# Lower parts, copies and operand sums put behind the work that the next products wait for

## The chip, the cores and the metric

The kernel runs on one core of a Trainium2 chip. The metric is the device time of one execution in microseconds; the time of a kernel is the median over its runs. One further execution is recorded by the hardware profiler, and all rows below come from that one.

The engines are named as in the profile: PE is the tensor engine (PEld its weight loads), DVE the vector engine, ACT the scalar engine, POOL the GpSimd engine, and SP the engine from whose queue nearly all transfers are issued.

## The reference

A decayed linear attention over blocks of 64 tokens, and then a two-layer feed-forward with a squared ReLU, everything in float32:

```python
for b in range(nb):
    intra = np.einsum('bhic,bhjc->bhij', qb, kb) * Dmask[None]
    intra = np.einsum('bhij,bhjd->bhid', intra, vb)
    inter = np.einsum('bhid,bhde->bhie', qb * lam_pow[None], kv_state)
    out[:, :, sl] = intra + inter
    kb_dec = kb * rev_pow[None]
    kv_state = lam_block[None, :, None, None] * kv_state + np.einsum('bhsd,bhse->bhde', kb_dec, vb)
...
h = x @ w_in
r = np.maximum(h, 0.0)
g = r * r
return (g @ w_out).astype(np.float32)
```

There are 4 sequences of 768 tokens, 8 heads of width 64, and a hidden width of 2048.

## The kernel before

**Precision.** A float32 product is made of three fast products: each operand is split into a high part (rounded, written by ACT or by a cast) and a lower part (the operand minus its high part, written by DVE), and high x high, high x low and low x high are added up. The helpers come in pairs: `part_hi`/`part_lo`, `rows_hi`/`rows_lo`, `fold_hi`/`fold_lo`, `weigh_hi`/`weigh_lo`. The `_hi` half runs on ACT, the `_lo` half on DVE. The tensors `wh` and `wl` hold the high and the lower parts of the weights, and later, in the same rows, those of other operands.

**Tiling.** The 3072 tokens are 24 chunks of 128 tokens, six per sequence, or six slices of four chunks. Slices 0 and 1 go through the feed-forward directly: for each of 16 hidden blocks f, `hidden` makes twelve products into a PSUM bank `h`, `square` (ACT) and `rest` (DVE) make `gh` and `gl` of it, and `project` of the previous block adds twelve products into four PSUM banks `acc`, one for each chunk. After the last block the four banks are copied out (tile `o`, two banks to a tile) and written to the output.

Slices 2 to 5 are done with seven products for every eight (sums of blocks of the operands are multiplied in place of the blocks). `quad(n)`, n = 0 to 7, opens the first pass over chunks 8 to 15, `gather_all(2, ...)` projects it, `quad_all(n, ...)` and `gather_all(4, ...)` do the same for chunks 16 to 23. I call `quad(0)` the first opening and `quad_all(0, ...)` the second. In an opening the products are numbered 0 to 6; products 0 and 4 go to bank `pa`, 1, 3 and 5 to `pb`, 2 and 6 to `pd`. After product 1 DVE adds `pb` and `p1` (a copy of product 0), after product 3 it does so again, and after product 4 it adds `pd` to that sum. Product 3 may start only when the first sum has read `pb`, product 5 when the second has, product 6 when `pd` has been read. The operand rows of the seven products are sums over chunks: `even` (rows 0 to 3), `last` (4 and 5), `near` (6 to 9), `far` (10 to 13).

**What runs beside it.** Slice 1 is the stretch in which all the preparation happens. At every even f, `go(t, t + 1)` runs the attention of one of the chunks 8 to 15: on PE the products with the old state (`old_state(0)`, L446), the scores of the next chunk (L411, into two banks `h`), the second half of the old state (`old_state(1)`, L446 again), and the products with the masked scores and the news for the state (L426). Between the first and the second half of the old state stands a one-element ACT copy (`mark`, L462), which PE waits for. `masked_by_half` (DVE, tile `a`) then multiplies the new scores by the mask; the next `hidden` reuses a bank of those scores, so PE's next twelve products wait for it. Beside that, in the same steps, the weights are recombined (`weigh`: tiles `rec`, `sums`, `parts`) and written to DRAM (`ws`), and the output weights are folded (`fold`: the same tile names, written to `wt`). POOL scales q, k and the state (`scale_q` L403, `scale_k` L395, `fade_state` L503).

**What sets the order.** Nothing is reordered by a scheduler: each engine runs its instructions in the order in which the Python code issues them, and waits in that order. A tile of a pool takes over the place of the tile of its tag that was released first, and waits for whatever still uses that. The tiles `rec`, `sums`, `near`, `far` and `o` share two places (tag `A`).

The calls at which the work stands, in the loop over f in slice 1:

```python
        for _, lo, x in now:
            lo(*x)
        if f == NF - 1:
            x = far(*pair(3))
            for a in (x, last(*pair(3))):
                part(*a)
        if f == 0:
            fold_hi(NQ - 2, True)
            fold_lo(NQ - 2)
        project(*prev)
        prev = (1, f)
        if f % 2 == 0:
            go(t, t + 1)
```

Of the kernel before, what the change touches and what calls it, by code (L numbers as in the profile page):

```python
# [35 lines left out]
def body(ctx: ExitStack, tc: tile.TileContext, qT, kT, kvq, lam, w, out):  # L36
# [399 lines left out]

    def go(t, after, own=None):
        po, pn = (ps_acc, "acc") if own is not None else (ps_a, "att")
# [23 lines left out]
        nc.scalar.copy(mark[:, 2:3], o[0][0:1, c : c + 1])  # L462
        u = o
        if after is not None:
            scores_by_half(after, qo, qn)
# [11 lines left out]
        if after is not None:  # L477
            part_of[after] = u[1]
            masked_by_half(after, own)
        x = kept(t).rearrange("p (a two c) -> p a two c", two=2, c=C)  # L480
        for h in range(2):
# [5 lines left out]

    def state(t, second):

        if not second and t % NCB == NCB - 1:  # L490
            return
        u = part_of.pop(t)[:, NPR * D :].rearrange("p (a b) -> p a b", a=NPR)
        d = kv[:, :, D:] if second else kv[:, :, 0:D]
        if second and not t % NCB:
            V.tensor_copy(d, u)
        else:
            add(d, kvd, u)
        if not second or t % NCB < NCB - 1:
            fade_state(second)
# [35 lines left out]
    def project(m, f):  # L535
        gh, gl = g_of.pop((m, f))
        if f == 0:
            accs[m] = [ps_acc.tile([P, DM], F32, name="acc") for _ in range(G)]
# [8 lines left out]
        def low(i):  # L547
            cs = slice(i * C, (i + 1) * C)
            nc.tensor.matmul(accs[m][i], gl[:, cs], wh[:, j], start=False, stop=end)  # L549
            if end:  # L550
                if i % 2 == 0:
                    stage.append(wk.tile([P, 2, DM], F32, name="o", tag="A"))
                o = stage[-1][:, i % 2]
                if i % 2 and not m:
                    V.tensor_copy(o, accs[m][i])
                else:
                    nc.scalar.copy(o, accs[m][i])
                t = chunk(m, i)
                nc.sync.dma_start(out=out[t * C : (t + 1) * C, :], in_=o)

        for i in range(G):
            high(i)
            low(i)

    def new_x(m):
# [202 lines left out]

    def quad(n, prev):
        f, t = 2 * n, 4 * G + n  # L770
# [24 lines left out]
        if n:  # L795
            square_pair(n - 1)
        product(n, 1, pb, True, False)
        add(gs[0], pb, p1)
        for e, i in MOVES.get(n, ()):
            move(e, spare(i))  # L800
# [81 lines left out]
    def quad_all(n, then):  # L882
# [25 lines left out]
        product(n, 3, pb, False, False)  # L908
        add(u3, pb, p1)
        product(n, 4, pa, False, True)  # L910
        add(gs[1], pd, u3)
# [201 lines left out]
    def late():  # L1113
        rows_lo(2, GT[0][:, 2:4])
        rows_of(6, GT[3][:, 2:4])
        rows_of(4, GT[1][:, 2:4])

# [161 lines left out]
    def behind(f, t):  # L1279
        if f % 2:  # L1280
            state(t, False)
            scale_q(t + 1)

    def ahead(f, t):
        if f % 2:
            state(t + 1, True)
            scale_k(t + 2)

# [9 lines left out]
    def pair(i):  # L1298
        return i, first_t + 2 * i

    todo = {f + 1: [(weigh_hi, weigh_lo, (n,))] for n, f in enumerate(WEIGH)}
    todo.setdefault(2, []).append((lambda n: fold_hi(n, True), fold_lo, (NQ - 3,)))
# [4 lines left out]
    for f in range(NF):  # L1307
# [14 lines left out]
        ahead(f, t)  # L1322
        for _, lo, x in now:
            lo(*x)
        if f == NF - 1:
            x = far(*pair(3))
            for a in (x, last(*pair(3))):
                part(*a)
        if f == 0:
            fold_hi(NQ - 2, True)  # L1330
            fold_lo(NQ - 2)
        project(*prev)
        prev = (1, f)
        if f % 2 == 0:
            go(t, t + 1)
            if t == last_t:
# [19 lines left out]
    for n in range(NF // 2):  # L1356
        quad(n, prev)
    for i, x in enumerate(GT):
# [61 lines left out]
```

## Time and profile before

| what | value |
|---|---|
| median of 3 runs | 580.46 us (580.02 to 581.17) |
| the profiled execution | 579.66 us, of which the span from the first to the last instruction is 578.0 us |
| PE busy | 566.7 us (98%) |
| DVE busy | 443.6 us (77%) |
| ACT busy | 299.2 us (52%) |
| POOL busy | 97.8 us (17%) |
| granted clock of PE | 1.000 over the whole span |

How to read it: PE is busy nearly all the time, and the granted clock never falls. The busy time of PE is modelled from the starts of its instructions, so what can be won without removing products is in the moments when PE waits. The other engines have slack on average, but not at every place.

### The profile page before, as it was taken

The page shows a single profiled execution, that of the slowest core. Times are in us where ns is not written, and L with a number is a line of the kernel's source. Part 1 is how long each engine was busy: PE and PEld are TensorE (multiplying, and loading weights), DVE is VectorE, ACT ScalarE, POOL GpSimd, SP SyncE. Part 2 cuts the span into 40 slices and gives each one's busy share as a digit, 9 for nine tenths or more (in the row PEclk, how much of TensorE's full clock was granted, in tenths as well). Part 3 has the DMA queues.
Part 4 walks back from the last instruction along what each step waited for, and adds up shares of the span by engine and source line. Part 5 has one row for each costly group of instructions (what it writes and reads, how often), then busy time and mean ns, then how long its engine had stood idle before and what let it go on. Part 6 is the DMA issues. An engine that isn't in the chain of part 4 may idle for free.

```text
span 578.0 us, 13430 instructions
## 1 busy us (share of the span) xinstructions
PE 566.7 (98%) x5308; PEld 494.1 (85%) x5308; DVE 443.6 (77%) x732; ACT 299.2 (52%) x524; POOL 97.8 (17%) x106
## 2 busy tenths in 40 slices
PE   9998999999999999999999999999999999999996
PEld 7886888887888888788888799999978888999996
DVE  5999999986887677767784699696865456997933
ACT  3777877834555555556675784153323234551510
POOL 4420221432313232322333000000000000000000
PEclk9999999999999999999999999999999999999999
DMA  8857485436699887499999776699678676767863
GB/s 302 325 173 259 151 285 186 143 128 239 220 292 362 284 271 258 133 315 366 370 392 357 257 229 214 204 293 330 196 243 258 197 192 194 237 216 208 284 203 109
DMA packets 87325, 142.69 MB, mean 247 GB/s; under 512 B 7776, under 2 KB 40544, under 8 KB 87264
## 3 DMA queue, kind: packets, MB, share of 16 engines
q1 hardware_dynamic: 82624, 136.61, 71.8%
q10 hardware_dynamic: 4640, 5.24, 2.5%
q8 instruction: 42, 0.69, 0.5%
q14 instruction: 19, 0.16, 0.1%
HBM read 106.96 MB, written 31.46 MB: 239 GB/s over the span
## 4 chain that ended last, share of the span: by engine, by line
PE 78%; DVE 9%; issue 5%; ACT 3%; DMA 3%; POOL 1%; SPq 1%; DVEq 0%; POOLq 0%; ACTq 0%
PE h L674 19%; PE acc L1007 16%; PE h L514 8%; PE att L1007 8%; PE att L674 7%; PE h L1007 4%; PE acc L544 2%; PE acc L549 2%; PE acc L545 2%; DMA ws<-parts 2%; PE acc L446 2%; DVE parts L214 1%; DVE sums L214 1%; DVE rec L214 1%; DMA kv_sb<-in_kvq 1%
## 5 line engine op out<-in xcount | busy, mean ns | idle before, releaser
L674 PE MATMUL h<-wh,ring 128*128 128x512 f32 x320 | 87.1, 394 | 1.8 <-DVE gs L214 1.0
L674 PEld LDWEIGHTS h<-wh,ring 128*128 128x128 f32 x320 | 59.1, 188 | 15.5 <-DVE gs L214 1.4
L1007 PE MATMUL acc<-folds,wh 128*128 128x256 f32 x384 | 70.5, 283 | 0.0
L1007 PEld LDWEIGHTS acc<-folds,wh 128*128 128x128 f32 x384 | 59.9, 192 | 0.0
L979 ACT CAST wh<-sums 128x1024 fp32r<-128x1024 f32 x32 | 33.6, 1050 | 45.5 <-DVE sums L214 17.6
L1007 PE MATMUL acc<-folds,wl 128*128 128x256 f32 x192 | 54.4, 283 | 0.0
L544 PE MATMUL acc<-wh,gh 128*128 128x512 f32 x128 | 50.3, 393 | 0.0
L549 PE MATMUL acc<-wh,gl 128*128 128x512 f32 x128 | 50.0, 390 | 0.0
L545 PE MATMUL acc<-wl,gh 128*128 128x512 f32 x128 | 49.9, 389 | 0.0
L674 PE MATMUL h<-wl,ring 128*128 128x512 f32 x160 | 49.4, 390 | 0.0
L214 DVE TENSOR_TENSOR wl<-sums,wh 128x1024 fp32r<-128x1024 f32 x37 | 45.0, 1217 | 2.9 <-ACT wh L979 2.9
L521 ACT ACTIVATE h<-h 128x512 f32<-128x512 f32 x32 | 18.6, 581 | 43.1 <-PE h L514 42.9
L529 DVE TENSOR_TENSOR gl<-h,gh 128x512 fp32r<-128x512 f32 x32 | 21.9, 686 | 21.6 <-ACT h L524 21.6
L503 POOL TENSOR_TENSOR kvd<-kv,qpow 128x256 f32<-128x256 f32 x27 | 21.1, 783 | 99.9 <-DVE kv L214 88.1
L1007 PEld LDWEIGHTS acc<-folds,wl 128*128 128x128 f32 x192 | 36.9, 192 | 0.0
L514 PE MATMUL h<-xh,wh 128*128 128x512 f32 x128 | 36.0, 403 | 0.6 <-DVE a L214 0.2
L514 PE MATMUL h<-xh,wl 128*128 128x512 f32 x128 | 34.5, 391 | 1.6 <-DVE wl L159 1.6
L674 PEld LDWEIGHTS h<-wl,ring 128*128 128x128 f32 x160 | 30.0, 188 | 6.4
L514 PE MATMUL h<-xl,wh 128*128 128x512 f32 x128 | 34.3, 390 | 0.0
L674 PE MATMUL att<-wh,ring 128*128 128x512 f32 x128 | 34.2, 389 | 0.0
L514 PEld LDWEIGHTS h<-xh,wl 128*128 128x128 f32 x128 | 24.0, 188 | 7.2 <-DVE wl L159 2.0
L860 ACT ACTIVATE h<-h 128x512 f32<-128x512 f32 x16 | 9.3, 581 | 39.3 <-PE h L674 32.1
(266 smaller groups left out, 1429.9 us busy)
## 6 DMA issues: line engine op xcount, KB each, us to landing
folds<-wt SPq DMA_DIRECT2D x128, 256.0 KB, 3.8
ring<-ws SPq DMA_DIRECT2D x112, 256.0 KB, 4.2
raw<-in_w SPq DMA_DIRECT2D x30, 512.0 KB, 4.3
kv_sb<-in_kvq SPq DMA_DIRECT2D x22, 512.0 KB, 6.1
ws<-parts SPq DMA_DIRECT2D x32, 256.0 KB, 4.7
qk_sb<-in_kT SPq DMA_DIRECT2D x22, 256.0 KB, 4.7
qk_sb<-in_qT SPq DMA_DIRECT2D x22, 256.0 KB, 5.3
out_x<-qk_sb ACTq DMA_DIRECT2D x16, 256.0 KB, 5.3
```

The source lines that it names most:

```text
L214: lambda o, x, y, op=op: V.tensor_tensor(out=o, in0=x, in1=y, op=op)
L446: nc.tensor.matmul(o[h][r, p * D : (p + 1) * D], x, y, start=(h, r.start) not in begun, stop=end, skip_group_check=True,)
L503: nc.gpsimd.tensor_tensor(out=kvd, in0=d, in1=qpow[:, :, D - 1 : D].broadcast_to([P, NPR, D]), op=ALU.mult)
L514: nc.tensor.matmul(h, wt[:, f, kt * P : (kt + 1) * P], x[:, kt], start=k == 0, stop=k == 11)
L521: nc.scalar.activation(h, h, AF.Relu)
L529: V.tensor_tensor(out=gl, in0=r, in1=gh.bitcast(F32), op=ALU.subtract)
L544: nc.tensor.matmul(accs[m][i], gh[:, cs], wh[:, j], start=f == 0, stop=False)
L545: nc.tensor.matmul(accs[m][i], gh[:, cs], wl[:, j], start=False, stop=False)
L549: nc.tensor.matmul(accs[m][i], gl[:, cs], wh[:, j], start=False, stop=end)
L674: nc.tensor.matmul(bank, x[:, part_, kt], t[:, q + kt], start=start and z == 0, stop=stop and z == 5, skip_group_check=True,)
L979: nc.scalar.copy(o_, x)
L1007: nc.tensor.matmul(bank[:, r * 2 * P : (r + 1) * 2 * P], x, y, start=k == 0 and r == 0 and z == 0, stop=k == NQ - 1 and z == 2, skip_group ...
```

## The change

It moves work within the queues of ACT, DVE, POOL and SP; no product, copy or sum is added or removed, but for one one-element POOL copy.

1. At f = 0 of slice 1, `project` now returns two functions, and `go` calls them: the high part of the folded sums is cast behind `mark`, and their lower part and the copies of the third and fourth bank stand behind the masked scores. The copies of the first two banks stay where they were.
2. At every even f the lower parts (`lo`) are made behind `go`, not ahead of `project`.
3. At the end of slice 1 the high and lower parts of `far` and the lower part of `last` of the fourth pair of chunks move into the first opening, behind product 1 (the high part) and behind the sum that follows it (the lower parts). The scaling of q and k and one fading of the state move there too, behind a one-element POOL copy that waits for the last lower part.
4. In the second opening the lower parts of rows 4 and 5 move from ahead of product 2 to behind the sum that follows product 3.

```diff
-    def go(t, after, own=None):
+    def go(t, after, own=None, ahead=None):
...
         nc.scalar.copy(mark[:, 2:3], o[0][0:1, c : c + 1])
         u = o
+        if ahead is not None:
+            ahead[0]()
         if after is not None:
             scores_by_half(after, qo, qn)
...
             masked_by_half(after, own)
+        if ahead is not None:
+            ahead[1]()
...
-    def state(t, second):
+    def state(t, second, fades=True):
...
-        if not second or t % NCB < NCB - 1:
+        if fades and (not second or t % NCB < NCB - 1):
             fade_state(second)
...
     def project(m, f):
         gh, gl = g_of.pop((m, f))
+        rest_ = []
...
             if end:
-                if i % 2 == 0:
-                    stage.append(wk.tile([P, 2, DM], F32, name="o", tag="A"))
-                o = stage[-1][:, i % 2]
-                if i % 2 and not m:
-                    V.tensor_copy(o, accs[m][i])
+                if i < 2 or m:
+                    leave(i)
                 else:
-                    nc.scalar.copy(o, accs[m][i])
-                t = chunk(m, i)
-                nc.sync.dma_start(out=out[t * C : (t + 1) * C, :], in_=o)
+                    rest_.append(i)
+
+        def leave(i):
+            if i % 2 == 0:
+                stage.append(wk.tile([P, 2, DM], F32, name="o", tag="A"))
+            o = stage[-1][:, i % 2]
+            if i % 2 and not m:
+                V.tensor_copy(o, accs[m][i])
+            else:
+                nc.scalar.copy(o, accs[m][i])
+            t = chunk(m, i)
+            nc.sync.dma_start(out=out[t * C : (t + 1) * C, :], in_=o)
+
+        def others():
+            fold_lo(NQ - 2)
+            for i in rest_:
+                leave(i)
...
+        return lambda: fold_hi(NQ - 2, True), others
...
         product(n, 1, pb, True, False)
+        if n == 0:
+            part_hi(*far_)
         add(gs[0], pb, p1)
+        if n == 0:
+            part_lo(*far_)
+            part_lo(*last_)
+            nc.gpsimd.tensor_copy(mark[:, 0:1], wl[0:1, 5, 3 * C : 3 * C + 1].bitcast(F32))
+            scale_q(t)
+            fade_state(True)
+            scale_k(t + 1)
...
         add(u3, pb, p1)
+        if then is not None:
+            rows_lo(4, GT[1][:, 2:4])
         product(n, 4, pa, False, True)
...
         rows_of(6, GT[3][:, 2:4])
-        rows_of(4, GT[1][:, 2:4])
+        rows_hi(4, GT[1][:, 2:4])
...
-        for _, lo, x in now:
-            lo(*x)
+        if f % 2:
+            for _, lo, x in now:
+                lo(*x)
         if f == NF - 1:
-            x = far(*pair(3))
-            for a in (x, last(*pair(3))):
-                part(*a)
-        if f == 0:
-            fold_hi(NQ - 2, True)
-            fold_lo(NQ - 2)
-        project(*prev)
+            part_hi(*last(*pair(3)))
+            rest_of_pair.append(far(*pair(3)))
+        mid = project(*prev)
         prev = (1, f)
         if f % 2 == 0:
-            go(t, t + 1)
+            go(t, t + 1, ahead=mid if f == 0 else None)
+            for _, lo, x in now:
+                lo(*x)
...
     for n in range(NF // 2):
-        quad(n, prev)
+        quad(n, prev, rest_of_pair[0], last(*pair(3)))
```

In `behind` and `ahead` the scaling of q and k and the second fading are left out at the last f (15); the first opening makes them up.

**Place 1: ACT at f = 0 of slice 1**, around the first attention. The first row is the last of the squares of f = 0; `parts<-sums` is the high part of the folded sums, `o<-acc` are the copies of the first and the third bank, `mark` is the copy that PE waits for, `raws` takes the attention's result. Before:

```order
L524 ACTIVATE h<-h 128x512
L716 CAST parts<-sums 128x1024 [waits DVE_49]
L557 COPY o<-acc 128x512 [waits PE_49]
L557 COPY o<-acc 128x512 [waits DVE_49,PE_49]
L462 COPY mark<-att 1x1 [waits PE_49]
L483 COPY raws<-att 128x2x64 [waits PE_49]
```

Now:

```order
L528 ACTIVATE h<-h 128x512
L568 COPY o<-acc 128x512 [waits DVE_49,PE_49]
L462 COPY mark<-att 1x1 [waits PE_49]
L733 CAST parts<-sums 128x1024
L568 COPY o<-acc 128x512 [waits DMAHW1_49,DMAHW2_49,DVE_49,Activation_49]
L487 COPY raws<-att 128x2x64 [waits PE_49]
```

Only one copy is left between the squares and `mark`. The copy of the third bank now waits for two transfers (DMAHW1 and DMAHW2): its tile takes the place of the tile of the first two banks, and those two transfers are its way to the output.

**Place 2: DVE at f = 4 of slice 1**, the first of the even steps with weights to split. `gl` is the lower part of the squares, `parts` the lower part of the weight sums, `a` the two masked copies, `rec` the next weights. Before:

```order
L529 TENSOR_TENSOR gl<-h,gh 128x512 [waits PE_49,Activation_49]
L214 TENSOR_TENSOR parts<-sums,parts 128x1024 [waits DMAHW5_49,DMAHW2_49,DMAHW6_49,DMAHW1_49,Activation_49]
L214 TENSOR_TENSOR a<-h,mask 128x256 [waits PE_49] x2
L214 TENSOR_TENSOR rec<-wh,wl 128x1024
L214 TENSOR_TENSOR sums<-rec 128x256 [waits DVE_49]
```

Now:

```order
L533 TENSOR_TENSOR gl<-h,gh 128x512 [waits PE_49,Activation_49]
L214 TENSOR_TENSOR a<-h,mask 128x256 [waits PE_49] x2
L214 TENSOR_TENSOR parts<-sums,parts 128x1024 [waits DMAHW5_49,DMAHW2_49,DMAHW6_49,DMAHW1_49,Activation_49]
L214 TENSOR_TENSOR rec<-wh,wl 128x1024
L214 TENSOR_TENSOR sums<-rec 128x256 [waits DVE_49]
```

The masked copies and the lower part have changed places; the lower part keeps its waits for transfers (it rewrites a tile that was written to DRAM two weights earlier), and `rec` still stands behind both.

**Place 3: DVE between slice 1 and the first opening.** `far<-raws` are the sums of the fourth pair, `wl<-far` and `wl<-raws` the lower parts of `far` and `last`, `gs<-h,p` the sums behind product 1 and product 3. Before:

```order
L214 TENSOR_TENSOR far<-raws 128x256
L214 TENSOR_TENSOR far<-far 128x256 [waits DVE_49]
L640 TENSOR_TENSOR wl<-far,wh 128x4x128 [waits Activation_49]
L640 TENSOR_TENSOR wl<-raws,wh 128x2x128 [waits Activation_49]
L214 TENSOR_TENSOR gs<-h,p_2791 128x512 [waits PE_49,Activation_49]
L214 TENSOR_TENSOR gs<-h,p_2791 128x512 [waits PE_49]
```

Now:

```order
L214 TENSOR_TENSOR far<-raws 128x256
L214 TENSOR_TENSOR far<-far 128x256 [waits DVE_49]
L214 TENSOR_TENSOR gs<-h,p_2785 128x512 [waits PE_49,Activation_49]
L657 TENSOR_TENSOR wl<-far,wh 128x4x128 [waits Activation_49]
L657 TENSOR_TENSOR wl<-raws,wh 128x2x128
L214 TENSOR_TENSOR gs<-h,p_2785 128x512 [waits PE_49]
```

The sum behind product 1 now stands ahead of both lower parts; it still stands behind the sums `far`.

## Rows read from the trace of the kernel before

**Rows 1.** Waits of PEld: line waited for: us in total, times, longest us

```profile
PEld h L674 <- DVE gs L214: 1.4, 1, 1.4
...
PEld att L446 <- ACT mark L462: 1.3, 1, 1.3
...
PEld h L674 <- ACT h L860: 1.2, 1, 1.2
PEld h L514 <- DVE a L214: 1.1, 4, 0.3
```

**Rows 2.** Timeline, f = 0: start us, us, instruction, count [idle before <-releaser]

```profile
133.41 0.46 PE L446 MATMUL att<-qk_sb,kv 64*64 64x64 f32 x16
...
135.48 0.46 PE L446 MATMUL att<-qk_sb,kv 64*64 64x64 f32 x16 [1.15 <-ACT mark L462]
...
136.81 1.20 PE L514 MATMUL h<-xh,wh 128*128 128x512 f32 x4
...
139.66 0.39 PE L544 MATMUL acc<-wh,gh 128*128 128x512 f32 x1
```

**Rows 3.** Timeline of ACT and DVE, f = 0

```profile
134.81 0.58 ACT L557 COPY o<-acc 128x512 f32<-128x512 f32 x1 [0.86 <-DVE parts L214]
135.29 0.14 ACT L462 COPY mark<-att 1x1 f32<-1x1 f32 x1
...
133.49 1.23 DVE L214 TENSOR_TENSOR parts<-sums,parts 128x1024 fp32r<-128x1024 f32 x1 [0.17 <-ACT parts L716]
```

**Rows 4.** Timeline of PE, f = 2: the same attention without a wait

```profile
147.91 0.46 PE L446 MATMUL att<-qk_sb,kv 64*64 64x64 f32 x16
...
149.97 0.50 PE L514 MATMUL h<-xh,wh 128*128 128x512 f32 x1
```

**Rows 5.** Line L559, the eight output transfers of slices 0 and 1

```profile
DMA to landing us min/median/max: 2.0/4.0/4.9
```

**Rows 6.** Timeline of DVE, f = 4

```profile
161.94 1.23 DVE L214 TENSOR_TENSOR parts<-sums,parts 128x1024 fp32r<-128x1024 f32 x1 [0.51 <-ACT mark L462]
163.08 0.75 DVE L214 TENSOR_TENSOR a<-h,mask 128x256 f32<-128x256 f32 x2
```

**Rows 7.** Busy times by window, 150 to 200 us; next to last is the DMA share

```profile
core 0: us, PE busy (x) PEld busy (x) DVE busy (x) ACT busy (x) POOL busy (x), PEclk, DMA share, GB/s
150.00:200.00 50.00, 49.60 (x542) 40.93 (x539) 38.12 (x62) 25.99 (x58) 15.08 (x14) 1.00 1.00 329
```

**Rows 8.** Timeline, f = 6: the scaled keys of the next chunk, and PE's use

```profile
173.46 1.07 POOL L395 TENSOR_TENSOR kv_sb<-kv_sb,mask 128x512 f32<-128x512 f32 x1 [4.63 <-DMA kv_sb<-in_kvq]
...
176.18 0.64 PE L426 MATMUL att<-kv_sb 64*64 64x64 f32 x16
```

**Rows 9.** Timeline of PE, first opening: products 2 and 3, and the attention

```profile
242.51 0.61 PE L674 MATMUL att<-wl,ring 128*128 128x512 f32 x2
244.10 1.19 PE L674 MATMUL h<-wh,ring 128*128 128x512 f32 x4 [0.98 <-DVE gs L214]
...
247.05 0.46 PE L446 MATMUL acc<-qk_sb,kv 64*64 64x64 f32 x16
```

**Rows 10.** Timeline of DVE, ACT and POOL, end of slice 1 and first opening

```profile
237.29 2.45 DVE L640 TENSOR_TENSOR wl<-far,wh 128x512 fp32r<-128x512 f32 x2
...
243.37 0.68 DVE L214 TENSOR_TENSOR gs<-h,p 128x512 f32<-128x512 f32 x1
...
241.77 0.62 ACT L636 CAST wh<-far 128x512 fp32r<-128x512 f32 x1 [5.38 <-DVE far L214]
...
239.16 1.50 POOL L395 TENSOR_TENSOR kv_sb<-kv_sb,mask 128x512 f32<-128x512 f32 x1
```

**Rows 11.** Timeline of DVE and PE, second opening

```profile
418.75 3.49 DVE L214 TENSOR_TENSOR wl<-gs,wh 128x1024 fp32r<-128x1024 f32 x3
422.15 0.68 DVE L214 TENSOR_TENSOR kv_sb<-h,p 128x512 f32<-128x512 f32 x1
...
421.50 0.61 PE L674 MATMUL h<-wl,ring 128*128 128x512 f32 x2
422.94 1.17 PE L674 MATMUL h<-wh,ring 128*128 128x512 f32 x4 [0.82 <-ACT h L860]
```

More of the change, by code (lines that the diff above doesn't have):

```diff
@@ L767, in body, with quad @@
     ROUNDED = {1: 4, 2: 0, 3: 1, 4: 2, 6: 3}
-    def quad(n, prev):
+    def quad(n, prev, far_, last_):
         f, t = 2 * n, 4 * G + n
@@ L1281, in behind @@
             state(t, False)
-            scale_q(t + 1)
+            if f < NF - 1:
+                scale_q(t + 1)
     def ahead(f, t):
         if f % 2:
-            state(t + 1, True)
-            scale_k(t + 2)
+            state(t + 1, True, f < NF - 1)
+            if f < NF - 1:
+                scale_k(t + 2)
     WEIGH = [2, 3, 4, 5, 6, 7, 9, 10]
@@ L1299, in pair @@
         return i, first_t + 2 * i
+    rest_of_pair = []
     todo = {f + 1: [(weigh_hi, weigh_lo, (n,))] for n, f in enumerate(WEIGH)}
```

## The prediction

> **What bounds the kernel now.** I read the page first: PE is busy 98% of the span at full clock, so with no product removed only PE's own waits can be won. The waits of PE's weight loads come next, because they name whom PE waits for. Four of their lines stand at places that the change touches: 1.4 us for a sum on DVE (first opening), 1.3 for `mark` (f = 0), 1.2 in the second opening, and 1.1 in four pieces for the masked scores at even f [rows 1]. Together 5.0 us of a span of 578.0: the ceiling of what shorter waits here can give. A listed wait overlaps products still in flight, so each size below comes from starts in the timeline at the place instead.
>
> **f = 0.** From the first product with the old state to the first product of the next `hidden` PE takes 136.81 − 133.41 = 3.40 us [rows 2]. The same chain at f = 2, without a wait, takes 149.97 − 147.91 = 2.06 [rows 4]. The difference is 1.34 us. Its cause stands on ACT: the copy of the third bank stands ahead of `mark` and idles 0.86 us for a lower part on DVE (133.49, 1.23 long); `mark` follows at 135.29 [rows 3]. Now `mark` comes right behind the first bank's copy, which does not wait for a lower part, so I take the whole 1.34 as returned. The masked scores lose the lower part ahead of them too.
>
> The price is the new wait: the copies of the third and fourth bank need the transfers of the first two to have read their tile. The second bank's copy takes the lower part's place on DVE at 133.49, and a copy of this shape takes about 0.6 (ACT's took 0.58 [rows 3]), so its transfer is issued near 134.1. Output transfers land 2.0 to 4.9 us later [rows 5]: 136.1 to 139.0. With 0.58 for the copy the third bank is free at 136.7 to 139.6. PE's next `project` starts at 139.66 − 1.34 = 138.3 and reaches the third bank six products later; twelve products take 139.66 − 136.81 = 2.85 [rows 2], so six take 1.4: 139.7. The cover holds at both ends, by 0.1 at the late one. Loss 0 (bound 0.9, if copy and transfer are each late by half a microsecond). Behind the waiting copy on ACT and DVE stand the attention's copies (`raws`) and the next squares; these get at most what the copy waits.
>
> **Even f.** The lower part stands ahead of the masked copies on DVE (f = 4: 161.94, 1.23 long; the copies from 163.08 [rows 6]), and PE's 1.1 us in four pieces is for those copies [rows 1]. With the order turned round they start up to 1.2 us sooner, longer than any piece (0.3). I take 1.1 back. The lower part comes 0.75 later, the length of the two masked copies [rows 6]. What hides that is DVE's idle time, 50 − 38.12 = 11.9 us between 150 and 200 [rows 7], and that nothing on PE reads these weights in this slice; without that cover it is 0.75 for each even step with a weight.
>
> PE itself now comes earlier, by 1.34 and most of the 1.1, so what it consumes must be ready. The nearest such operand that I found is the scaled keys at f = 6: ready at 173.46 + 1.07 = 174.53, read at 176.18 [rows 8]. That leaves 1.65 against a lead of about 1.34 + 0.4 there, 0.4 being the piece or two before it. A shortfall of 0.1 at most; I take 0.
>
> **First opening.** Product 3 could start when product 2's last two weight loads are through: 242.51 + 2 × 0.23 = 242.97, with 0.23 from 0.46 for 16 small or 2.85 for twelve full products [rows 2]. It starts at 244.10 [rows 9]: 1.13 us. The sum that it waits for runs at 243.37 for 0.68 [rows 10], behind the lower parts. In the new order it stands right behind the sums `far`, which end where ACT's cast of them starts, at 241.77 [rows 10]: 241.8 + 0.7 = 242.45, ahead of 242.97. So 1.13 comes back whole.
>
> Three followers. The high part of `far` now waits on ACT for nothing new (241.77 + 0.62 = 242.4). The lower parts follow the sum, 242.45 + about 0.7 = 243.1 for `far`, and a last one behind it; product 3 runs its high products first, and its last two of six come at 242.97 + 4 × 0.23 = 243.9: covered. POOL's three operations now wait for the last lower part, near 243.6. At no more than 1.50 each [rows 10] they end by 245.1, 246.6 and 248.1. PE's attention, now at 247.05 − 1.13 = 245.9 [rows 9], needs the first (queries) at once, and the last (keys) only after its products with the old state and the scores, about 1.5 later (247.4). Loss 0 to 0.7. I take 0, since POOL moving away also speeds DVE up: two lower parts of 512 took 2.45 beside POOL's work [rows 10], where three of 1024 took 3.49 without it [rows 11], that is 0.58 for 512 each. All that follows on DVE would then be up to 2.45 − 1.16 = 1.3 earlier, and POOL would be done by 246.8.
>
> **Second opening.** Product 3 could start at 421.50 + 0.46 = 421.96 and starts at 422.94 [rows 11]: 0.98 us. The profile names an ACT copy there [rows 1], but DVE's sum (422.15 + 0.68 = 422.83) ends 0.11 before PE restarts, so I take the sum. Three lower parts from 418.75 hold it up [rows 11]. With the third behind it, it runs from 418.75 + 2 × 1.16 = 421.07 to 421.75: before 421.96. The third lower part then ends near 422.9, and the sum behind product 4, which frees bank `pd` for product 6, near 423.6. PE wants `pd` at 421.96 + 6 × 0.23 = 423.3: products 4 and 5 fill less than I would like, so there is a new wait of 0.2 to 0.3. Net 0.98 − 0.25 = 0.73, between 0.5 (the new wait doubled) and 0.98 (none).
>
> **The sum.** 1.34 + 1.1 + 1.13 + 0.73 = 4.3. The span goes from 578.0 to 573.7; the profiled execution, 1.66 longer than its span, from 579.66 to 575.36. The median of the runs lies 0.80 above that execution, so the median to expect is 576.16, say **576.2**. What a measurement of this kernel can tell from no change is about 0.2%, 1.2 us.
>
> **The rivals.**
> *The output transfer at f = 0 is late.* If it lands later than 4.9 us, or its issue is held up on SP, each microsecond beyond costs PE one, since the third bank is written in order. With 1.5 lost: 577.7. For it: 0.1 of cover at the late end. Against: the median landing is 4.0 [rows 5].
>
> *DVE and POOL collide in the even steps.* The moved lower parts could fall beside POOL's scaling, as those of 237.29 did (1.29 us lost [rows 10]). A hit would push `rec`, then the next step's lower squares, and PE waits for those instead of the masked copies: 1.1 not returned, 1.29 lost, 578.6. Against it: 11.9 us of idle DVE [rows 7]. The Trainium skill, "SBUF — State Buffer", section "Who interferes with whom", says that a VectorE instruction with two SBUF inputs contends with a GpSimd instruction that reads SBUF, and one with at most one such input does not. The trace agrees for the lower parts of `far` (2.45 against 1.16); by that rule the masked copies, with scores from PSUM beside the mask, are never held, while the moved lower parts can be, which speaks for this rival's mechanism and not for its price.
>
> *The releasers are misnamed.* If the second opening waits for the ACT copy named, and the even steps for something that the order of DVE does not move (the scores' own end on PE, say), only 1.34 + 1.13 come back: 578.0. For it: the name in [rows 1]; against: the 0.11 between sum and restart.
>
> *The transfers are the bound in slice 1 (the other side).* The DMA share from 150 to 200 is 1.00 [rows 7]. If that stream is saturated, the weights written 0.75 later in each of about five even steps are never caught up, and the loads behind them in SP's queue (the next chunk's q, k and v) come 3.75 later. The keys have 1.65 to spare [rows 8]; from there PE waits, and the first two terms are not returned: 580.46 + 3.75 − 1.13 − 0.73 = 582.35. Against it: POOL waits 4.63 us for those loads and PE none [rows 8]; the delay would have to add up and not be taken in by a gap. With less than half of it the result is no change.
>
> *More than the sum.* With the lower squares no longer behind a lower part, short unlisted waits go as well, and the new wait in the second opening is absent: 575.2 or a little less.
>
> **How the numbers follow.** Forecast 0.62, more than the sum 0.06, late output 0.04, collisions 0.10, misnamed releasers 0.10, transfers as the bound 0.08 (half no change, half slower). The forecast's own range is 575.6 to 577.0: the losses bounded above on one side (0.7 of POOL, 0.2 of the second opening), on the other the new wait gone and a spread of runs of some tenths. The whole range goes from 575.0, under the better case, to 578.6, the collisions' price; outside are the last rival and tails of the others. Faster by over 0.2%: 0.62 + 0.06 + 0.04 + 0.10 + 0.10 = 0.92; within: 0.04; slower: 0.04.
>
> **What the profile after would show.** Right: at f = 0 the chain is 2.06 long, `mark` idle only for PE, and an ACT copy of the third bank idle behind a DMA; no PE wait for masked scores of over 0.1; product 3 of the first opening right behind product 2, and POOL's scaling behind 243; in the second opening the first sum ahead of the third lower part and a wait of 0.2 to 0.3 at product 6. Wrong: a wait of `acc` for the copies at f = 0, of the openings' attention for POOL, of `project` for lower squares, or of PE for `kv_sb` at f = 6 or later, each with its own size.

## The result and the profile after

| | median of the runs (us) | profiled execution's span (us) |
|---|---|---|
| before | 580.37 (5 runs, 579.60 to 581.17) | 578.0 |
| changed | 575.51 (5 runs, 574.62 to 575.89) | 574.0 |

The ratio is 0.9915, 95% interval 0.9902 to 0.9929: 4.1 to 5.7 us faster, 4.86 by the medians. (The five runs of before are the three told of above and two more.) Forecast were 576.2, with a range of 575.0 to 578.6.

The first view is again the list of PE's waits, here of the weight loads of the changed kernel (the line, whom it waited for, us in total, times, longest):

```profile
PEld h L518 <- DVE wl L159: 1.9, 1, 1.9
...
PEld att L691 <- ACT kept L887: 0.4, 1, 0.4
...
PEld acc L554 <- DVE gl L533: 0.3, 1, 0.3
PEld h L411 <- DVE gl L533: 0.2, 1, 0.2
```

The four lines of [rows 1] are gone. The first row stands in slice 0, which the change doesn't touch. The second row (`kept`) is the new wait at product 6 of the second opening; the list names an ACT instruction there, but DVE's order decides it (lo_last below). What else is left at the changed places is small: lower squares (`gl`).

The timeline of PE, ACT and DVE at f = 0 (start, duration, instruction, count, idle time before and its releaser), to be read beside [rows 2] and [rows 3]:

```profile
133.54 0.46 PE L446 MATMUL att<-qk_sb,kv 64*64 64x64 f32 x16
134.29 0.44 PE L446 MATMUL att<-qk_sb,kv 64*64 64x64 f32 x16
...
135.60 1.20 PE L518 MATMUL h<-xh,wh 128*128 128x512 f32 x4
...
134.07 0.15 ACT L462 COPY mark<-att 1x1 f32<-1x1 f32 x1 [0.92 <-PE att L446]
134.13 1.04 ACT L733 CAST parts<-sums 128x1024 fp32r<-128x1024 f32 x1
136.28 0.59 ACT L568 COPY o<-acc 128x512 f32<-128x512 f32 x1 [1.11 <-DMA out_x<-o]
```

The chain takes 135.60 − 133.54 = 2.06 us, as long as the one without a wait [rows 4]. ACT now waits for PE ahead of `mark`, not the other way round. The copy of the third bank idles 1.11 us behind a transfer, as its new wait says, and ends at 136.87; PE's products of the third bank come at 139.82. So 2.95 us of cover (139.82 − 136.87) were left in this execution.

The first opening, PE, DVE and POOL, beside [rows 9] and [rows 10]:

```profile
240.65 0.61 PE L691 MATMUL att<-wl,ring 128*128 128x512 f32 x2
241.10 1.07 PE L691 MATMUL h<-wh,ring 128*128 128x512 f32 x4
...
235.65 1.29 DVE L657 TENSOR_TENSOR wl<-far,wh 128x512 fp32r<-128x512 f32 x2
...
237.98 0.68 DVE L214 TENSOR_TENSOR gs<-h,p 128x512 f32<-128x512 f32 x1
238.75 0.69 DVE L657 TENSOR_TENSOR wl<-far,wh 128x512 fp32r<-128x512 f32 x1
...
239.84 0.17 POOL L821 COPY mark<-wl 1x1 f32<-1x1 f32 x1 [4.57 <-DVE wl L657]
...
241.81 1.05 POOL L395 TENSOR_TENSOR kv_sb<-kv_sb,mask 128x512 f32<-128x512 f32 x1
```

Product 3 starts right behind product 2, 2.4 us after the sum that it needs. Two lower parts of `far` take 1.29 in place of 2.45, since POOL's work no longer runs beside them (pool_back below brings the 2.45 back).

The second opening, PE and DVE, beside [rows 11]:

```profile
418.39 0.62 PE L691 MATMUL h<-wl,ring 128*128 128x512 f32 x2
418.85 1.10 PE L691 MATMUL h<-wh,ring 128*128 128x512 f32 x4
419.79 0.62 PE L691 MATMUL h<-wl,ring 128*128 128x512 f32 x2
420.43 1.17 PE L691 MATMUL att<-wh,ring 128*128 128x512 f32 x4
...
417.91 0.69 DVE L214 TENSOR_TENSOR kv_sb<-h,p 128x512 f32<-128x512 f32 x1
418.51 1.22 DVE L214 TENSOR_TENSOR wl<-gs,wh 128x1024 fp32r<-128x1024 f32 x1
419.64 0.69 DVE L214 TENSOR_TENSOR gs<-att,kv_sb 128x512 f32<-128x512 f32 x1
```

The sum starts at 417.91 and ends at 418.60, ahead of the end of product 4's loads; the wait of 0.98 is gone. The third lower part now stands ahead of the sum that frees bank `pd`, which ends at 420.33; product 6 starts at 420.43, 0.64 us behind the start of product 5's last two, where 0.46 is the rule (418.39 to 418.85): the new wait, at the place that the prediction gave it.

PE executes the same products in the same order in all kernels here, so stretches can be compared from start to start. **f = 0** is from the first product with the old state to the first of the next `hidden`; **even f** from there to the first product of `hidden` behind the attention of f = 14; **first** from there to product 3 of the first opening; **between** from there to the second opening; **second** is the second opening, up to the next one's first product. All in us, worked out from the starts in the traces; the runs are those told of below:

```
kernel          f = 0   even f   first   between   second
before           3.40    93.74   13.55    171.02    10.65
before_again     3.40    93.77   13.57    171.05    10.61
changed          2.06    93.12   12.38    170.92     9.87
after_again      2.06    93.62   12.38    170.92     9.88
undo_f0          3.41    92.59   12.39    170.96     9.87
undo_even        2.06    93.93   12.37    170.65     9.87
undo_first       2.06    92.35   13.76    171.62     9.85
undo_second      2.06    92.99   12.37    170.67    10.66
pool_back        2.06    92.92   12.37    170.65     9.87
lo_last          2.06    92.85   12.39    170.64     9.55
cast_ahead       2.05    93.35   12.37    170.65     9.87
late_out         2.06    93.03   12.37    170.88     9.85
best             2.06    96.84   12.38    170.92     9.55
best_free        2.06    96.72   12.41    171.41     9.55
```

From the row of before to that of the changed kernel: 1.34 + 0.62 + 1.17 + 0.10 + 0.78 = 4.0. The spans differ by as much within 0.1: f = 0 begins at 133.54 in place of 133.41. Neither that nor the 0.10 of `between` is from a place that the change touches.

### The profile page after: what moved, and what is told of

It reads as the page before. It is cut to its first block, busy times and chain, and to the rows that moved or that the text cites. A ratio compares the mean times of both kernels' runs of the same rounds, so it can differ in the third digit from the quotient of the medians.

```text
span 574.0 us, 13432 instructions
## 1 busy us (share of the span) xinstructions
PE 565.0 (98%) x5308; PEld 492.8 (86%) x5308; DVE 441.9 (77%) x732; ACT 299.4 (52%) x524; POOL 95.4 (17%) x107
## 4 chain that ended last, share of the span: by engine, by line
PE 87%; DMA 5%; DVE 5%; ACT 1%; issue 1%; SPq 1%; DVEq 0%; ACTq 0%
PE h L691 19%; PE acc L1035 16%; PE h L518 12%; PE att L1035 8%; PE att L691 8%; PE acc L549 4%; PE h L1035 4%; PE acc L554 4%; PE acc L550 4%; PE acc L446 2%; DMA lent<-in_qT 1%; PE att L446 1%; DMA ws<-parts 1%; DMA kv_sb<-in_kvq 1%; DMA qk_sb<-in_qT 1%
```

## The experiments

All are edits of the changed kernel; ratios are to the kernel before, each with its 95% interval.

**undo_f0, undo_even, undo_first, undo_second: one part undone at a time.**

```diff
 # undo_f0
+        if f == 0:
+            fold_hi(NQ - 2, True)
+            fold_lo(NQ - 2)
-        mid = project(*prev)
+        project(*prev)
...
 # undo_even
-        if f % 2:
-            for _, lo, x in now:
-                lo(*x)
+        for _, lo, x in now:
+            lo(*x)
...
 # undo_first
-            part_hi(*last(*pair(3)))
-            rest_of_pair.append(far(*pair(3)))
+            x = far(*pair(3))
+            for a in (x, last(*pair(3))):
+                part(*a)
...
 # undo_second
-        rows_hi(4, GT[1][:, 2:4])
+        rows_of(4, GT[1][:, 2:4])
```

(undo_f0 also copies all four banks in `project` again, undo_first takes back the code of the first opening and the conditions in `behind` and `ahead`.)

> The changed kernel with the part at f = 0 undone. Theory (the four parts stand by themselves): the chain from the first product with the old state at f = 0 to the next hidden takes 3.4 us again, PE is 1.34 us later from there to the end, span about 1.3 longer than the changed kernel's, time 576.8. Rival (the parts lean on each other): the changed kernel waits for lower squares at f = 4 and 8 because it is early; with PE 1.34 later these short waits go, and only 0.6 to 0.9 is lost by the first opening, time 576.2.

> The changed kernel with the lower parts of even f ahead of project and go again. Theory: the waits for the masked scores at f = 4, 8, 10, 14 come back, 0.80 us by starts, the wait of the scores at f = 4 (0.16) goes: 0.64 us longer between f = 2 and the first opening, time 576.15. Rival: the prediction's own 1.1 us, read from the list of waits of PE's weight loads, was right and something else took 0.5 of it: 1.1 longer, time 576.6.

> The changed kernel with the end of slice 1 and the first opening as before. Theory: product 3 waits again for the sum behind the lower parts, 1.2 to 1.3 us, time 576.8; nothing else moves. Rival: since PE now arrives 1.8 us sooner at this place and DVE's sums do not, the stall grows to 2 us or more, time 577.5.

> The changed kernel with the lower parts of rows 4 and 5 ahead of product 2 again. Theory: the wait of product 5 of the second opening (the product that the prediction calls 3) comes back with 0.95 to 1.05 us, the wait of 0.26 at product 6 goes, 0.75 longer, time 576.25. Rival: the ACT copy named by the list of waits is what ends it, and the wait stays away: time 575.5.

| run | median (us) | ratio | interval |
|---|---|---|---|
| undo_f0 | 576.34 | 0.9934 | 0.9921 to 0.9947 |
| undo_even | 576.25 | 0.9936 | 0.9924 to 0.9947 |
| undo_first | 576.41 | 0.9941 | 0.9928 to 0.9953 |
| undo_second | 575.55 | 0.9926 | 0.9909 to 0.9942 |

The whole times cannot price the single parts. Against the ratio 0.9915 of the changed kernel they are 0.19, 0.21, 0.26 and 0.11% longer, together 0.77%; against the 0.9927 of its repetition (after_again, below) 0.07, 0.09, 0.14 and none, together 0.3%; and the intervals overlap. By its time alone undo_second (575.55; 576.25 expected, 575.5 by its rival) would even speak for its rival, and undo_f0 (576.34) is nearer to its rival (576.2) than to its theory (576.8). The stretches, which repeat within 0.04 at three of the four places (before_again and after_again, below), decide.

undo_f0 has 3.41 at f = 0 again. Its even f (92.59) is 0.53 shorter than in the changed kernel's first profile, 0.32 of it because the wait for lower squares at f = 4 is gone, as the rival said. But that wait is gone in undo_first as well (92.35), where PE is not later there, so that the part at f = 0 brings it about is not shown.

undo_second has 10.66: the wait comes back, with the same wrong name in the list of PE's waits, although only DVE's order was changed:

```profile
PEld h L691 <- ACT h L886: 1.2, 1, 1.2
```

That settles the prediction's doubt about the releaser: the sum on DVE it is. undo_first has 13.76, 1.38 more than the changed kernel, where 1.2 to 1.3 were expected and 2 by the rival; its `between` is also longer (below). undo_even has 93.93, which is 0.81 more than the changed kernel's first profile, where 0.64 was expected and 1.1 by the rival: nearer to the theory, and between the two. Its list shows 1.6 us for the masked scores:

```profile
PEld h L518 <- DVE a L214: 1.6, 6, 0.3
```

By starts of PE's instructions these six places (f = 4 to 14) lose 1.1 us against the changed kernel, and the whole stretch is 1.0 longer than the mean below: the list of waits is too large by about half.

**pool_back: POOL's three operations stay at the end of slice 1.**

```diff
-            nc.gpsimd.tensor_copy(mark[:, 0:1], wl[0:1, 5, 3 * C : 3 * C + 1].bitcast(F32))
-            scale_q(t)
-            fade_state(True)
-            scale_k(t + 1)
...
```

(The conditions on the last f in `behind` and `ahead` go too.)

> The changed kernel with POOL's scaling of q and k and the fading back at the end of slice 1, and without the one-element copy; DVE and ACT keep the new order. Theory (the place of the first sum in DVE's queue returned the stall): two lower parts of far take about 2.4 again in place of 1.3, the sum behind product 1 ends 1 to 2 us later, near 240.6 at the latest, and product 3 still wants it only at 241.1: no loss above 0.2 us, time 575.5. Rival (POOL's move returned it): product 3 waits 0.5 to 1.1 us again, time 576.3.

575.20, ratio 0.9921 (0.9907 to 0.9935); `first` 12.37: nothing is lost. DVE, PE and POOL there:

```profile
235.14 2.46 DVE L657 TENSOR_TENSOR wl<-far,wh 128x512 fp32r<-128x512 f32 x2
...
239.52 0.68 DVE L214 TENSOR_TENSOR gs<-h,p 128x512 f32<-128x512 f32 x1
...
240.60 1.07 PE L691 MATMUL h<-wh,ring 128*128 128x512 f32 x4
...
237.02 1.50 POOL L395 TENSOR_TENSOR kv_sb<-kv_sb,mask 128x512 f32<-128x512 f32 x1
```

Beside POOL the lower parts take 2.46 again, and the sum ends at 240.20, 0.4 us ahead of product 3 (2.4 in the changed kernel). The order on DVE returned the stall; moving POOL's work bought 2 us of cover and no time.

**lo_last: the lower parts of rows 4 and 5 one sum later.**

```diff
-        if then is not None:
-            rows_lo(4, GT[1][:, 2:4])
         product(n, 4, pa, False, True)
         add(gs[1], pd, u3)
+        if then is not None:
+            rows_lo(4, GT[1][:, 2:4])
```

> The changed kernel with the lower parts of rows 4 and 5 one sum later, behind the sum that frees the bank of product 6. Theory: that sum ends near 419.2 and product 6 starts right behind product 5, so the wait of 0.26 us goes; the lower part ends near 420.4, ahead of product 6's fifth product (421.1). Time 575.25. Rival: product 6 then waits for the lower part at its fifth product, or for ACT, and the 0.26 stays: 575.5.

575.11, ratio 0.9915 (0.9902 to 0.9929); `second` 9.55 in place of 9.87. PE and DVE:

```profile
418.97 0.62 PE L691 MATMUL h<-wl,ring 128*128 128x512 f32 x2
419.42 1.07 PE L691 MATMUL att<-wh,ring 128*128 128x512 f32 x4
420.33 0.62 PE L691 MATMUL att<-wl,ring 128*128 128x512 f32 x2
...
417.85 0.69 DVE L214 TENSOR_TENSOR gs<-att,kv_sb 128x512 f32<-128x512 f32 x1
418.45 1.22 DVE L214 TENSOR_TENSOR wl<-gs,wh 128x1024 fp32r<-128x1024 f32 x1
```

Product 6 starts 0.45 behind product 5's last two, and the row of `kept` is gone from the list of PE's waits. The lower part ends (419.67) before product 6's last third (420.33). So the new wait was the lower part's place, and 0.32 us more are to be had; a whole time of 575 does not resolve them.

**cast_ahead: the high part's cast ahead of `mark` again, alone.**

```diff
+        if f == 0:
+            fold_hi(NQ - 2, True)
         mid = project(*prev)
...
-        return lambda: fold_hi(NQ - 2, True), others
+        return lambda: None, others
```

> The changed kernel with only the cast of the folded sums' high part ahead of mark again; the lower part and the third and fourth bank's copies stay behind the masked scores. Theory (the wait for a lower part behind the third copy was the cause): ACT runs squares, cast and one copy without a gap, mark starts near 134.15 in place of 134.07: at most 0.15 us lost, time 575.6. Rival (the 1.04 us of the cast on ACT were the cause): about 1.0 lost, time 576.5.

576.15, ratio 0.9934 (0.9921 to 0.9947). At f = 0 nothing is lost (2.05): the cast was never the cause, the wait behind the third copy was. But one attention later, at f = 2, the chain takes 149.10 − 146.50 = 2.60 us in place of 2.06. ACT, DVE and PE:

```profile
138.71 0.59 ACT L568 COPY o<-acc 128x512 f32<-128x512 f32 x1 [4.69 <-DMA out_x<-o]
...
140.75 0.58 ACT L525 ACTIVATE h<-h 128x512 f32<-128x512 f32 x1
...
146.51 0.68 DVE L533 TENSOR_TENSOR gl<-h,gh 128x512 fp32r<-128x512 f32 x1
...
147.25 0.69 PE L411 MATMUL h<-qk_sb 64*64 64x64 f32 x30 [0.19 <-DVE gl L533]
```

Here the third copy waited 4.69 us for the outputs, to 138.71, where it was 136.28 in the changed kernel. The bank was still free in time (139.30, wanted at 139.61), but ACT's next squares stood behind it (140.75 in place of 138.66), DVE's work behind those, and PE waited for the lower squares of f = 2. So the late output cost PE its time by another way than the prediction's first rival has it: not by the third bank, but by the squares behind its copy. Of these 2.4 us only 0.26 come from the issue: the first bank's copy stands behind the cast, so SP issues the second output at 134.34 in place of 134.08. The other 2.2 are the transfer itself: it lands 4.3 us after its issue, in place of 2.1 in the changed kernel. The longest of the eight outputs of cast_ahead is this one:

```profile
DMA to landing us min/median/max: 2.0/2.5/4.3
```

The write of the folded sums is issued 0.44 us behind it (134.78), where the changed kernel has 1.11 (135.19). That the two transfers hold each other up is a guess that fits; one profile does not show it.

**late_out: the first two outputs issued behind the lower part.**

```diff
+            if not m and i < 2:
+                held_.append((t, o))
...
             fold_lo(NQ - 2)
+            for t, o in held_:
+                nc.sync.dma_start(out=out[t * C : (t + 1) * C, :], in_=o)
```

> The changed kernel with the output transfers of the first two banks at f = 0 issued behind the transfers of the folded sums, that is behind the lower part, near 136.5 in place of 133 to 134. Theory (the third and fourth copies wait for these transfers to land): landing 2.0 to 4.9 us later, at 138.5 to 141.4, the third copy 0.6 behind it, and PE wants the bank at 139.8: 0 to 2.2 us lost, 1.3 at the median landing of 4.0, time 576.8. Rival (the bank's cover is larger than the profile shows, or the transfer frees its tile long before it lands): 0 lost, time 575.5.

575.43, ratio 0.9920 (0.9907 to 0.9934); no loss anywhere. It missed its aim: with the later transfers the pool gives the third bank's copy another place, and it waits for the lower part alone, while the next weights (`rec`) wait for the transfers, without harm:

```profile
136.27 0.59 ACT L568 COPY o<-acc 128x512 f32<-128x512 f32 x1 [1.29 <-DVE parts L214]
...
142.10 1.29 DVE L214 TENSOR_TENSOR rec<-wh,wl 128x512 f32<-128x512 f32 x2 [0.88 <-DMA out_x<-o]
```

So the price of a late output was not measured on purpose; cast_ahead's 0.54 at a copy 2.4 us later is all there is.

**after_again, before_again: both kernels once more.** No edit.

> The changed kernel once more, unchanged. Theory (the four terms are the same in every execution but the one of the even f, which depends on when POOL's scaling falls beside DVE's sums): the stretch from f = 0's second half of the old state to the end of f = 14 lasts between 93.6 and 94.5 us (94.43 in the first profile), the three other places repeat within 0.1, time 575.5. Rival (the 0.64 of the even f in the first profile is the rule): 94.4 within 0.1.

> The kernel before once more, unchanged. Theory: the stalls of 1.34, 1.14 and 0.98 repeat within 0.1, and the even-f stretch lasts about 95.1 (95.07 in the first profile); time 580.2. Rival (the stretch varies by itself by half a microsecond and more): below 94.6 or above 95.6.

575.51, ratio 0.9927 (0.9915 to 0.9938), and 580.07, ratio 1.0002 (0.9992 to 1.0012). Three of the stretches repeat within 0.04. The even f of before repeat as well (93.74, 93.77), those of the changed kernel don't: 93.12 and 93.62. The theory expected 94.5 at most by its own measure, from f = 0's second half of the old state, and 94.93 came, so it fell short. The cause is the time at which POOL's scaled keys are ready for PE, not POOL's place beside DVE's sums. PE and POOL at f = 12 of after_again show it:

```profile
214.70 0.29 PE L426 MATMUL att<-kv_sb 64*64 64x64 f32 x4
215.22 0.68 PE L426 MATMUL att<-kv_sb 64*64 64x64 f32 x28 [0.23 <-POOL kv_sb L395]
...
214.11 1.06 POOL L395 TENSOR_TENSOR kv_sb<-kv_sb,mask 128x512 f32<-128x512 f32 x1 [4.54 <-DMA kv_sb<-in_kvq]
```

The scaled keys end at 215.17, 0.47 after this line's first product, and PE loses 0.5 there, which is the whole difference between the even f of the two profiles; in the changed kernel's first profile they were 0.06 ahead (213.77 + 1.06 = 214.83, used at 214.89), in the kernel before 1.63 (213.88 + 1.06 against 216.57).

**best, best_free: the weight sums and their cast behind the masked scores too** (with lo_last; best_free with late_out as well).

```diff
...
             go(t, t + 1, ahead=mid if f == 0 else None)
+            for x in sums_:
+                weigh_sums(*x)
+                weigh_hi(*x)
             for _, lo, x in now:
                 lo(*x)
```

> The changed kernel with the lower parts of rows 4 and 5 behind the sum that frees the bank of product 6, and at every even f with the weight sums and their cast behind the masked scores too, so that the lower squares stand ahead of them on DVE. Theory (what is left of the waits at even f is for lower squares that stand behind the sums): the even-f stretch shrinks from 94.2 to 93.4 to 93.7, the second opening by 0.3: time 574.5. Rival (the sums done later hold up the next odd f's lower squares): 94.2 or longer, time 575.2 or more.

> The same, and the output transfers of the first two banks at f = 0 are issued behind the lower part, by which the third bank's copy takes another place and waits for no transfer. Theory: the same time as the kernel ahead of it in this list, 574.5, within 0.3, with no copy on ACT idle behind a transfer at f = 0. Rival: the next weights' sums, which now take the outputs' place and wait for them, push the lower squares of f = 2 back, and 0.4 to 0.9 is lost at f = 2.

579.65, ratio 1.0001 (0.9992 to 1.0010), and 580.17, ratio 1.0002 (0.9992 to 1.0013): all that the change returned is lost again, at even f alone (96.84 and 96.72). DVE, POOL and PE of best, f = 10 to 12:

```profile
206.29 1.23 DVE L214 TENSOR_TENSOR parts<-sums,parts 128x1024 fp32r<-128x1024 f32 x1 [2.03 <-ACT parts L617]
...
217.09 1.40 POOL L395 TENSOR_TENSOR kv_sb<-kv_sb,mask 128x512 f32<-128x512 f32 x1 [3.00 <-DMA kv_sb<-in_kvq]
...
218.54 0.68 PE L426 MATMUL att<-kv_sb 64*64 64x64 f32 x28 [1.09 <-POOL kv_sb L395]
```

In the changed kernel that lower part runs at 201.81: here it is 4.5 us later. Its writes stand ahead of the next chunk's loads in SP's queue, and the load of the keys is issued later, here in best and then in the changed kernel:

```profile
210.76 0.38 SPq L89 DMA_DIRECT2D kv_sb<-in_kvq  x1
...
207.89 0.38 SPq L89 DMA_DIRECT2D kv_sb<-in_kvq  x1
```

The scaling of the keys starts at 217.09 in place of 213.77, and PE waits for them. By starts PE loses 2.8 us to the keys against the changed kernel (f = 8, 10 and 12). That is the mechanism of the prediction's last-but-one rival, in a kernel that delays the lower parts by 4.5 us and not by 0.75. It is not all: 1.6 us more are lost at the scores of f = 6 and 12, where PE waits for lower squares and, at f = 12, for `mark`, and 0.6 come back elsewhere. best_free, in which none of the copies at f = 0 waits for a transfer, shows the same.

## Why the prediction was right, point by point

**Right with their sizes:** f = 0 (forecast 1.34, measured 1.34; the new wait cost nothing), the first opening (1.13; 1.17, and undone 1.38; POOL in time, though pool_back shows that its move was not needed), the second opening (0.73; 0.78, with the new wait at product 6: 0.32 by lo_last, forecast 0.2 to 0.3). One name is wrong there: the product that the prediction calls 3 in the second opening is product 5. The rows and the arithmetic are those of product 5, which is why they hold. The 0.23 of a full product is right by the 2.85 for twelve; the 0.46 for 16 small ones, which the prediction names beside it, is the length of one row and says nothing on full products.

**Off in size: the even f.** The term of 1.1 was taken from the list of waits [rows 1], although the text says that sizes come from starts. By starts the four places (f = 4, 8, 10 and 14) give back 0.17 to 0.23 each, 0.84 together, and they do so in all nine profiles with this part and without the late sums. Measured over the whole stretch: 0.62 in the first profile; over the eight executions that have this part and neither the late sums nor cast_ahead's late copy the stretch is 92.35 to 93.62, mean 92.93, which is 0.82 less than the two of before. Two things make it vary. At f = 4 a weight sum ran beside POOL's scaling in the first profile and took 1.28 in place of 0.42, and the lower squares behind it came late; PE's scores lost 0.32 there. DVE and POOL:

```profile
158.51 1.28 DVE L214 TENSOR_TENSOR sums<-rec,sums 128x256 f32<-128x256 f32 x1
159.72 0.68 DVE L533 TENSOR_TENSOR gl<-h,gh 128x512 fp32r<-128x512 f32 x1
...
158.28 1.23 POOL L395 TENSOR_TENSOR kv_sb<-kv_sb,mask 128x512 f32<-128x512 f32 x1 [2.03 <-DMA kv_sb<-in_kvq]
```

The kernel before has this too, with 0.19 lost by the scores:

```profile
158.53 1.17 DVE L214 TENSOR_TENSOR sums<-rec 128x256 f32<-128x256 f32 x1
```

So 0.13 of the shortfall is from here; in undo_f0 and undo_first no sum is caught, and nothing is lost. It is the mechanism of the collisions' rival in small, but with a weight sum, not with a moved lower part. The rule of the Trainium skill that the prediction names ("SBUF — State Buffer", "Who interferes with whom") agrees with this and with 2.46 against 1.29 for the lower parts of `far`.

The other is f = 12, and here the prediction's step was wrong: it took the keys of f = 6 (1.65 to spare) as the nearest and the lead at that place. Those of f = 12 had 1.63 in the kernel before:

```profile
213.88 1.06 POOL L395 TENSOR_TENSOR kv_sb<-kv_sb,mask 128x512 f32<-128x512 f32 x1 [2.44 <-DMA kv_sb<-in_kvq]
...
216.57 0.69 PE L426 MATMUL att<-kv_sb 64*64 64x64 f32 x32
```

PE now comes to them with more lead, since three of the four places lie ahead: by the same sum 1.34 + 0.67 = 2.0, so 0.4 short. In the ten profiles of the changed kernel and of its edits without the late sums, the keys of f = 12 were between 1.76 us ahead and 0.47 late. So the loss that the rival of the saturated stream foretold, PE waiting for `kv_sb`, came in one of two profiles of the changed kernel, at 0.5 us; that writes made 0.75 later add up, which was that rival's reason, is not shown.

**Off in the last step: the median.** By the four places the sum is 3.9 in the first profile, and 4.1 with the mean of the even f, both less than the 4.3 forecast; yet the medians differ by 4.86. So 575.51 lies a little under the forecast's own range (575.6 to 577.0), on the side of the rival "more than the sum", but not for that rival's reasons: the new wait in the second opening was there, and the sum of the places was smaller, not larger. The prediction kept the 0.80 between the median and the profiled execution, a figure from three runs; over the 29 runs of before in the last comparison the median is 580.07, only 0.41 above that execution. The changed kernel's profiled execution lay 0.29 above its median (575.80 against 575.51). So the start of the sum was 0.4 too high and the sum itself 0.2 to 0.4 too large. In the forecast the two errors offset each other, which is luck. Why the changed kernel's median came out lower still is not shown; the difference is of the size of the spread of the runs. The repetition, 580.07 to 575.51 = 4.56, lies between; what makes single executions slower than the profiled ones was not looked into.

## What to carry to other kernels

Size a wait by what the next instructions' starts lose against the same chain without it, not by the list of waits, which came out larger than what the starts lose (1.1 against 0.84, 1.6 against 1.1) and named an ACT instruction twice where DVE's order decided. When PE becomes earlier, list the slack of every operand that a transfer brings at every repetition of the loop, not at one: the tightest of several equal places takes the gain away, and one profile shows its slack only for one execution. Delaying work behind which a queue's transfers stand is free only up to that slack: 0.75 us of delay was free or cost tenths, 4.5 us (with the sums delayed too) cost nearly the whole gain. What lies between was not tried.

## What the runs showed of the hardware that was not expected

`between` varies by 1.0 us over the executions, with equal products and no named wait. In undo_first 0.75 of it, by starts, is one wait of PE at the last product of an attention. The profile counts 0.54 of that as idle and names no releaser:

```profile
315.09 0.27 PE L426 MATMUL acc<-kv_sb 64*64 64x64 f32 x1 [0.54 <-issue]
```

The kernel before and best_free also lose 0.2 and 0.5 at this very product against the others, the repetition of before does not. Most of the rest, about 0.27 between two kinds of executions, comes in portions of 0.03 to 0.04 us, each spread over the dozen products right behind an attention; the two profiles of the changed kernel have it, lo_last and pool_back do not. What PE waits for in either stays open.
